# Loading q four tokens to a partition in two partition halves, with whole stores, in a linear-attention and feed-forward kernel

## Chip, cores and metric

One core of one Trainium2 chip. The metric is device time in microseconds (us). A run has a state: "fast", or "slow" where it lies over 1.5% above the fastest of its kernel; only fast runs are compared. A ratio below is the mean time of one kernel's fast runs over the mean of the other's fast runs of the same rounds, with a 95% interval; it is therefore not quite the ratio of the medians quoted beside it. "Span" is the time of the one profiled execution, some 2 to 3 us shorter than its timed run. In profile lines PE is TensorE, PEld its weight loads, DVE VectorE, ACT ScalarE, POOL GpSimd; `out<-in` names tiles, xN counts instructions, and L282 is a line of the kernel. "Granted clock" is the share of TensorE's full clock that it got.

## The reference

Decayed linear attention over blocks of 64 tokens, followed by a feed-forward layer whose activation is h + sin(ah)^2/a. There are 4 batches, 8 heads, 768 tokens and 64 dimensions a head; the feed-forward layer has 3072 rows, 512 wide, 2048 hidden.

```python
for b in range(nb):                                   # blocks of 64 tokens
    intra = np.einsum('bhic,bhjc->bhij', qb, kb) * Dmask[None]       # lam ** (i - j), i >= j
    intra = np.einsum('bhij,bhjd->bhid', intra, vb)
    inter = np.einsum('bhid,bhde->bhie', qb * lam_pow[None], kv_state)   # lam ** (i + 1)
    out[:, :, sl] = intra + inter
    kv_state = lam_block[None, :, None, None] * kv_state + np.einsum('bhsd,bhse->bhde', kb_dec, vb)
...
h = x @ w_in
s = np.sin(alpha * h)
return ((h + s * s / (alpha + 1e-09)) @ w_out).astype(np.float32)
```

## The kernel before

The work is cut into 24 units (256 tokens of one batch and four heads). A unit loads 256 KB each of q, k and v, scales q and k by powers of lam into bf16 (tiles QL and KD), transposes both, and runs the small matmuls of attention. Four units make one of six groups of 512 rows for the feed-forward layer. A list, ORDER, gives the program order of every operation; each engine takes its own in that order. Units 0 to 7 are transposed by TensorE, units 8 to 23 by DMA. All loads of q, k and v, all DMA transposes and nearly all stores are issued by one engine, the sync engine (SP; "SPq" in a profile is its DMA issues); I call that the sync queue. The DMAs that the sync engine and ScalarE issue take eight semaphores in turn, and a DMA waits until the eighth before it has landed: in the traces of the two kernels 255 of 260 DMAs whose eighth predecessor has a recorded landing carry that one's semaphore, and none was issued before that landing. I say that issues run free where those of a kind take their shortest time: in the kernel before a whole load's took 0.37 to 0.51 us in the first microseconds (up to 3.3 us) and again from 30.3 to 32.4 us.

```python
    def load(u, j, **_):                              # j: q, k or v
        ...
        tl = stagep.tile([P, HH, 2, D], FP32, name=f"st_{nm}")
        loads[u, j] = nc.sync.dma_start(              # 512 B pieces: two tokens of a head
            out=tl[:].rearrange("p h two e -> p h (two e)"),
            in_=src[b, hh * HH:(hh + 1) * HH, tp * W:(tp + 1) * W, :]
            .rearrange("h (p two) e -> p h (two e)", two=2))
        ...
    def turn_dma(u, j):
        nc.sync.dma_start_transpose(
            out=qkt[u][:, j].rearrange("p par hp i -> p (par hp) i"),
            in_=cast[u, "qk"[j]][:].rearrange("p par h e -> p (par h e)"))
    ...
    def outev(u, c, eng, **_):                        # attention result to the feed-forward input
        copy(eng, xt[g][:, 2 * hh:2 * hh + 2, bb, c, :],
             okv[u][c][:, 0:2 * P].rearrange("p (hp i) -> p hp i", hp=2))
    ...
    def store(g, m, par, **_):                        # even rows and odd rows: two half stores
        nc.sync.dma_start(out=out_rows(g, m)[par], in_=obs[g, m][par * D:(par + 1) * D, :])
```

Of the kernel before, what the change touches and what calls it, by code (L numbers as in the profile page):

```python
# [51 lines left out]
tdq.9:S s.8:T a.8.0:G sk.10:G st.0.0.0:S ld.12.0:S tdk.9:S st.0.0.1:S stt.1.6:V stt.1.7:V sin.1.8:A  # L52
sqr.1.8:A sin.1.9:A sin.1.10:A stt.1.8:V m.8.0:V f1.1.11:T:3 f1.1.12:T:0 f1.1.13:T:1 sq.11:G
tdq.10:S sin.1.11:A f1.1.14:T:4 ld.12.1:S ld.12.2:S ld.13.0:S sqr.1.9:V sqr.1.10:A sqr.1.11:G
stt.1.9:V stt.1.10:V sin.1.12:A sqr.1.12:G sin.1.13:A stt.1.11:V stt.1.12:V m.8.1:V sk.11:G
f1.1.15:T:2 cv.10:G sin.1.14:A sqr.1.13:A oi.8:T sin.1.15:A tdk.10:S f2.1.0.0:T:3 sqr.1.14:A sk.12:G
sq.12:G f2.1.0.1:T f2.1.0.2:T a.9.0:G sqr.1.15:A cv.11:A stt.1.13:V stt.1.14:V stt.1.15:V s.9:T
o.8:T tdq.11:S ld.13.1:S ld.13.2:S k.10:T:0,1 x.8.0:A x.8.1:A m.9.0:V tdk.11:S f2.1.0.3:T m.9.1:V
oi.9:T kc.10.0:A st.0.1.0:S ld.14.0:S kc.10.1:A o.9:T cv.12:A x.9.0:A s.10:T k.11:T:2,0 f2.1.1.0:T:1
m.10.0:V a.10.0:G x.9.1:A kc.11.0:A kc.11.1:A m.10.1:V oi.10:T k.12:T:2,0 n.6.0:G n.8.0:G n.9.0:G  # L60
s.11:T o.10:T kc.12.0:V f2.1.1.1:T ld.14.1:S m.11.0:V ld.14.2:S n.10.0:G x.10.0:V m.11.1:V
f2.1.1.2:T ld.15.0:S st.0.1.1:S ld.15.1:S tdq.12:S ld.15.2:S ld.16.0:S ld.16.1:S ld.16.2:S ld.17.0:S
oc.1.0:A kc.12.1:A x.10.1:A a.11.0:G sk.13:G cv.13:G oi.11:T o.11:T x.11.0:A sq.13:G f2.1.1.3:T
sq.14:G oc.1.1:A n.7.0:G x.11.1:V f1.2.0:T:6 sin.2.0:A f1.2.1:T:5 sin.2.1:A sqr.2.0:A stt.2.0:V
ld.17.1:S st.1.1.0:S a.6.1:G n.6.1:G sk.14:G ld.17.2:S st.0.3.0:S st.0.2.0:S f1.2.2:T:2 sin.2.2:A
sqr.2.1:A stt.2.1:V f1.2.3:T:7 sin.2.3:A f1.2.4:T:0 f1.2.5:T:3 sin.2.4:A f1.2.6:T:4 f1.2.7:T:5
sqr.2.2:G stt.2.2:V sqr.2.3:A a.5.1:G stt.2.3:V sin.2.5:A f1.2.8:T:6 f1.2.9:T:7 f1.2.10:T:1 sq.15:G
sk.15:G sqr.2.4:A sin.2.6:A sqr.2.5:A stt.2.4:V f2.1.2.0:T:0 stt.2.5:V cv.14:G f1.2.11:T:3 tdk.12:S
f1.2.12:T:2 sin.2.7:A f2.1.2.1:T st.0.2.1:S sin.2.8:A sqr.2.6:G sqr.2.7:A stt.2.6:V sin.2.9:A
stt.2.7:V sqr.2.8:G sin.2.10:A n.11.0:G stt.2.8:V sqr.2.9:A sqr.2.10:A stt.2.9:V stt.2.10:V sq.16:G  # L70
sin.2.11:A sqr.2.11:A tdq.13:S n.5.1:G tdk.13:S tdq.14:S st.0.3.1:S tdk.14:S a.7.1:G a.12.0:G s.12:T
k.13:T:6,7 kc.13.0:A sin.2.12:A kc.13.1:A sqr.2.12:A m.12.0:V m.12.1:V tdq.15:S f1.2.13:T:1
f2.1.2.2:T sin.2.13:A sqr.2.13:A oi.12:T s.13:T o.12:T stt.2.11:V f2.1.2.3:T a.13.0:G m.13.0:V
stt.2.12:V m.13.1:V stt.2.13:V x.12.0:A x.12.1:A f2.1.3.0:T:3 n.13.0:G n.7.1:G a.8.1:G oi.13:T
sk.16:G oc.1.2:A f1.2.14:T:2 o.13:T k.14:T:1,0 s.14:T sin.2.14:A x.13.0:V x.13.1:V m.14.0:V n.8.1:G
sq.17:G n.12.0:G kc.14.0:A f2.1.3.1:T m.14.1:V f2.1.3.2:T sqr.2.14:A a.14.0:G kc.14.1:A tdk.15:S
ld.18.0:S ld.18.1:S oi.14:T ld.18.2:S sq.18:G cv.15:A cv.16:G cv.17:A k.15:T:1,0 o.14:T s.15:T
tdq.16:S tdk.16:S stt.2.14:V kc.15.0:V x.14.0:V x.14.1:A f1.2.15:T:2 f2.1.3.3:T st.1.2.0:S a.15.0:G
m.15.0:V kc.15.1:V oi.15:T m.15.1:V ld.19.0:S ld.19.1:S ld.19.2:S s.16:T ld.20.0:S st.1.0.0:S o.15:T
x.15.0:V k.16:T:1 x.15.1:V sin.2.15:A sqr.2.15:A m.16.0:V oc.1.3:V stt.2.15:V a.11.1:G f2.2.0.0:T:0  # L80
f1.3.0:T:7 kc.16.0:A st.1.0.1:S ld.20.1:S m.16.1:V sin.3.0:A sqr.3.0:A f1.3.1:T:4 f1.3.2:T:6
sin.3.1:A f1.3.3:T:1 sqr.3.1:A sin.3.2:A sin.3.3:A f1.3.4:T:5 sin.3.4:A f1.3.5:T:2 f1.3.6:T:3
sk.17:G st.1.2.1:S ld.20.2:S sk.18:G sk.19:G f2.2.0.1:T f2.2.0.2:T a.9.1:G sq.19:G sq.20:G sqr.3.2:G
stt.3.0:V sqr.3.3:A stt.3.1:V a.16.0:G n.9.1:G sin.3.5:A sqr.3.4:A stt.3.2:V n.14.0:G n.15.0:G
sin.3.6:A stt.3.3:V stt.3.4:V sqr.3.5:A ld.21.0:S tdq.17:S tdk.17:S sqr.3.6:A cv.18:G tdq.18:S
tdk.18:S st.1.3.0:S f1.3.7:T:1 oi.16:T stt.3.5:V a.10.1:G s.17:T o.16:T x.16.0:V k.17:T:2 f2.2.0.3:T
cv.19:G m.17.0:V stt.3.6:V x.16.1:V kc.17.0:A f2.2.1.0:T:2 a.17.0:G n.10.1:G n.11.1:G sk.20:G
cv.20:G a.12.1:G f2.2.1.1:T tdq.19:S ld.21.1:S tdk.19:S ld.21.2:S ld.22.0:S st.1.1.1:S tdq.20:S
ld.22.1:S tdk.20:S m.17.1:V oi.17:T oc.2.0:V s.18:T st.1.3.1:S k.18:T:3 k.19:T:0 o.17:T kc.18.0:A
f2.2.1.2:T a.18.0:G sin.3.7:A x.17.0:A x.17.1:A n.12.1:G f2.2.1.3:T m.18.0:V m.18.1:V f1.3.8:T:3  # L90
oi.18:T oc.2.1:V sqr.3.7:A sin.3.8:A sqr.3.8:A sq.21:G ld.22.2:S ld.23.0:S st.2.1.0:S sk.21:G
kc.19.0:V s.19:T o.18:T k.20:T:2 kc.20.0:A m.19.0:V stt.3.7:V f1.3.9:T:0 m.19.1:V f1.3.10:T:4
sin.3.9:A stt.3.8:V a.19.0:G f1.3.11:T:1 st.2.0.0:S x.18.0:A x.18.1:V sqr.3.9:G sk.22:G sin.3.10:A
sqr.3.10:A f1.3.12:T:3 f1.3.13:T:2 oi.19:T stt.3.9:V sin.3.11:A sqr.3.11:A sin.3.12:A stt.3.10:V
cv.21:A f2.2.2.0:T:0 f2.2.2.1:T f2.2.2.2:T stt.3.11:V a.20.0:G sqr.3.12:A sin.3.13:A o.19:T s.20:T
f1.3.14:T:1 x.19.0:A sqr.3.13:G sq.22:G x.19.1:V sin.3.14:A m.20.0:V stt.3.12:V f1.3.15:T:6
f1.4.0:T:7 sqr.3.14:G stt.3.13:V stt.3.14:V sin.3.15:A sin.4.0:A sqr.3.15:A sqr.4.0:A stt.3.15:V
stt.4.0:V tdq.21:S st.2.0.1:S ld.23.1:S f2.2.2.3:T oc.2.2:A f1.4.1:T:4 a.13.1:G cv.22:G sin.4.1:A
sqr.4.1:G m.20.1:V f1.4.2:T:3 f1.4.3:T:0 sin.4.2:A sin.4.3:A sqr.4.2:A sqr.4.3:A sq.23:G
f2.2.3.0:T:1 f2.2.3.1:T tdk.21:S tdq.22:S ld.23.2:S oi.20:T n.13.1:G f2.2.3.2:T f2.2.3.3:T o.20:T  # L100
k.21:T:2 stt.4.1:V s.21:T stt.4.2:V stt.4.3:V kc.21.0:V oc.2.3:A f2.3.0.0:T:0 f1.4.4:T:3 f2.3.0.1:T
f1.4.5:T:2 x.20.0:A sin.4.4:A sin.4.5:A sqr.4.4:G a.15.1:G sqr.4.5:G stt.4.4:V m.21.0:V m.21.1:V
stt.4.5:V f1.4.6:T:1 sin.4.6:A tdk.22:S tdq.23:S sqr.4.6:A stt.4.6:V a.21.0:G st.2.3.0:S f2.3.0.2:T
f1.4.7:T:6 f1.4.8:T:3 f2.3.0.3:T sk.23:G oc.3.0:V f1.4.9:T:1 f1.4.10:T:5 f1.4.11:T:4 x.20.1:V
sin.4.7:A sin.4.8:A sqr.4.7:G sqr.4.8:G stt.4.7:V stt.4.8:V cv.23:A f1.4.12:T:2 tdk.23:S st.3.0.0:S
sin.4.9:A sqr.4.9:A stt.4.9:V sin.4.10:A sqr.4.10:G stt.4.10:V f2.3.1.0:T:3 f2.3.1.1:T n.15.1:G
sin.4.11:A st.2.2.0:S st.2.1.1:S sqr.4.11:A stt.4.11:V oi.21:T o.21:T k.22:T:0 k.23:T:1 s.22:T
x.21.0:V m.22.0:V x.21.1:V m.22.1:V f2.3.1.2:T f2.3.1.3:T oc.3.1:V st.2.3.1:S a.14.1:G n.14.1:G
kc.22.0:A a.22.0:G oi.22:T o.22:T s.23:T m.23.0:V f2.3.2.0:T:0 f2.3.2.1:T x.22.0:V kc.23.0:A
x.22.1:A m.23.1:V a.23.0:G oi.23:T f2.3.2.2:T f1.4.13:T:3 o.23:T x.23.0:V f1.4.14:T:4 x.23.1:V  # L110
f1.4.15:T:1 sin.4.12:A sqr.4.12:A stt.4.12:V sin.4.13:A st.2.2.1:S st.3.0.1:S sin.4.14:A sqr.4.13:A
# [8 lines left out]
stt.5.11:V stt.5.12:V st.4.0.0:S st.3.2.0:S st.3.2.1:S st.3.3.0:S st.3.1.0:S st.3.3.1:S f1.5.15:T:7  # L120
sin.5.13:A sin.5.14:A st.3.1.1:S f2.4.1.3:T oc.4.1:V sqr.5.13:A sqr.5.14:G sin.5.15:A stt.5.13:V
stt.5.14:V f2.4.2.0:T:4 st.4.0.1:S st.4.1.0:S st.4.1.1:S sqr.5.15:G stt.5.15:V f2.4.2.1:T f2.4.2.2:T
f2.4.2.3:T f2.4.3.0:T:0 f2.4.3.1:T f2.4.3.2:T f2.4.3.3:T f2.5.0.0:T:3 f2.5.0.1:T f2.5.0.2:T oc.4.2:V
oc.4.3:A st.4.3.0:S st.4.2.0:S st.4.3.1:S st.4.2.1:S f2.5.0.3:T oc.5.0:V st.5.0.0:S st.5.0.1:S
f2.5.1.0:T:2 f2.5.1.1:T f2.5.1.2:T f2.5.1.3:T f2.5.2.0:T:5 f2.5.2.1:T f2.5.2.2:T oc.5.1:V f2.5.2.3:T
st.5.1.0:S st.5.1.1:S lt.0:T:3 oc.5.2:V st.5.2.0:S lt.1:T:7 st.5.2.1:S ltc.0:A lt.2:T:5 ltc.1:A
ltc.2:V
"""

@with_exitstack  # L130
def kernel(
    ctx: ExitStack,
# [61 lines left out]
    nc.scalar.activation(out=warm[:], in_=warm[:], func=ACTF.Sin)  # L194
    alpha_r = consts.tile([NFC, P], FP32, name="alpha_r")
    nc.scalar.dma_start(out=alpha_r[:], in_=moe_alpha.rearrange("(f p) -> f p", p=P))

    pos = consts.tile([P, 1], FP32, name="pos")
    jt = consts.tile([P, 2], FP32, name="jt")
    for c in range(2):  # L200
# [54 lines left out]
    def load(u, j, **_):  # L255
# [7 lines left out]
        if (u, j) == (4, 0):  # L263
            after(loads[u, j], f1mm[HOLD])
# [25 lines left out]
    def table(eng, **_):  # L290
        tabs.append(ps.tile([P, 2, 2, H], FP32, name="tab", tag="h3", bufs=1))
        for j, t in enumerate((E, R)):
            copy(eng, tabs[0][:, j], t[:])
# [332 lines left out]
```

## Time and profile before

| what | before | how to read it |
|---|---|---|
| time | 217.48 us, median of 3 (215.25 to 217.53) | 216.37 with the run beside the changed kernel |
| span of the profile | 213.8 us | TensorE busy 204.0 us, 95% |
| first feed-forward matmul | 18.43 us | end of the start |
| last DMA transpose ends | 151 us | after it the sync queue only stores |
| sync queue issuing, 30 to 120 us | 89 to 94% of the time | issue times of the trace added up in 15 us windows |

### The profile page before, as it was taken

Reading aid. Unit: us, or ns where it says so; the run is one execution under the profiler, and the core shown is the slowest. Engines: PE = TensorE matmul, PEld = TensorE weight load, DVE = VectorE, ACT = ScalarE, POOL = GpSimd, SP = SyncE. Lnnn points to the kernel's source line nnn. Section 1 sums busy time; section 2 is a strip of 40 time slices with the busy share of each in tenths; the row PEclk is TensorE's granted clock in tenths of the full one; section 3 lists DMA queues with packets and bytes.
Section 4 is the critical chain, followed back from the end, with each engine's and each line's share of the span. In section 5 each row is a group of like instructions: output and inputs, shape, how many; then the busy total and the mean of one; then the engine's idle time right before and its main releaser. Section 6 shows DMA issues by size and latency. Waiting matters only on the chain.

```text
span 213.8 us, 5465 instructions
## 1 busy us (share of the span) xinstructions
PE 204.0 (95%) x2104; PEld 110.1 (51%) x2132; DVE 129.8 (61%) x235; ACT 123.5 (58%) x244; POOL 141.4 (66%) x208
## 2 busy tenths in 40 slices
PE   7989999999999999999799999999999999999993
PEld 5767544457744554455444554454454444444463
DVE  3885798159599845778667785626884626441120
ACT  3563984077899839986394496936635659131001
POOL 5488389689797999999898996709841728030000
PEclk9999999999999999999999999999999999999999
DMA  5999999999999999989899997520610000171624
GB/s 144 293 235 196 187 204 271 282 291 289 200 205 202 248 213 289 208 103 199 218 268 133 223 179 198 92 49 0 132 44 3 0 0 0 35 179 35 147 51 98
DMA packets 64009, 33.92 MB, mean 159 GB/s; under 512 B 19680, under 2 KB 61040, under 8 KB 63984
## 3 DMA queue, kind: packets, MB, share of 16 engines
q1 hardware_dynamic: 59568, 29.31, 62.5%
q0 software_dynamic: 4224, 4.19, 12.4%
q8 instruction: 16, 0.26, 0.5%
q10 hardware_dynamic: 192, 0.07, 0.2%
q14 instruction: 9, 0.07, 0.1%
HBM read 27.28 MB, written 6.29 MB: 157 GB/s over the span
## 4 chain that ended last, share of the span: by engine, by line
PE 67%; POOL 12%; DMA 10%; issue 3%; ACT 2%; SPq 2%; DVE 2%; POOLq 0%; ACTq 0%
PE ops L525 27%; PE hps L482 24%; DMA w_out_sb<-in_moe_w_out_dram 4%; PE bz L564 3%; DMA QT<-KD 2%; PE okv L460 2%; POOL KD L300 2%; POOL kvbd L425 2%; PE sp L368 2%; PE bz L588 2%; DMA st_v<-in_v_dram 2%; POOL QL L300 2%; POOL kvx L421 2%; PE pt L327 2%; SPq L259 2%
## 5 line engine op out<-in xcount | busy, mean ns | idle before, releaser
L482 PE MATMUL hps<-xt,w_in_sb 128*128 128x512 bf16 (+1 forms) x404 | 86.4, 362 | 0.6 <-issue 0.2
L525 PE MATMUL ops<-w_out_sb,gall 128*128 128x512 bf16 x352 | 83.2, 379 | 2.1 <-issue 1.3
L516 DVE SCALAR_TENSOR_TENSOR gall<-s,r_sb,hps 128x512 bf16<-128x512 bf16 x96 | 68.3, 744 | 23.3 <-POOL s L511 11.7
L502 ACT ACTIVATE s<-hps,alpha_sb 128x512 bf16<-128x512 f32 x96 | 63.2, 688 | 25.7 <-PE hps L482 25.1
L482 PEld LDWEIGHTS <-w_in_sb 128*128 128x128 bf16 x416 | 39.8, 98 | 40.6
L511 POOL TENSOR_TENSOR s<-s 128x512 bf16<-128x512 bf16 x35 | 36.3, 1045 | 36.3 <-ACT s L502 35.6
L525 PEld LDWEIGHTS <-gall 128*128 128x128 bf16 x368 | 34.6, 98 | 39.9 <-issue 0.6
L378 DVE TENSOR_TENSOR ST<-sp,mask 128x512 bf16<-128x512 f32 x48 | 31.9, 684 | 4.4 <-PE sp L368 4.2
L509 ACT ACTIVATE s<-s 128x512 bf16<-128x512 bf16 x51 | 31.6, 634 | 1.0 <-DVE gall L516 0.4
L284 DVE COPY ob<-ops 128x512 f32<-128x512 f32 (+1 forms) x13 | 8.6, 659 | 29.2 <-PE ops L525 23.6
L300 POOL TENSOR_TENSOR QL<-st_q,E 128x512 bf16<-128x512 f32 x23 | 23.9, 1042 | 3.6 <-DVE alpha_sb L574 2.2
L300 POOL TENSOR_TENSOR KD<-st_k,R 128x512 bf16<-128x512 f32 x22 | 22.9, 1042 | 3.5 <-DMA st_k<-in_k_dram 1.8
L425 POOL TENSOR_TENSOR kvbd<-kvx,LBD 128x256 bf16<-128x256 f32 x32 | 19.6, 612 | 2.5
L282 ACT COPY ob<-ops 128x512 f32<-128x512 f32 (+2 forms) x13 | 7.1, 547 | 22.4 <-PE ops L550 12.0
L282 ACT CAST xt<-okv 128x256 bf16<-128x256 f32 x29 | 9.8, 374 | 11.8 <-PE okv L460 11.8
L421 POOL TENSOR_TENSOR kvx<-kva,kvs 128x128 f32<-128x128 f32 x32 | 14.7, 460 | 1.2 <-ACT kva L282 1.0
L284 DVE CAST xt<-okv 128x256 bf16<-128x256 f32 x19 | 7.7, 420 | 11.5 <-PE okv L460 11.5
L282 ACT COPY kva<-kvp 128x128 f32<-128x128 f32 x26 | 6.4, 273 | 9.9 <-PE kvp L400 8.9
L368 PE MATMUL sp<-QT 64*64 64x128 bf16 x384 | 9.9, 219 | 1.3 <-DMA QT<-KD 1.3
L282 ACT COPY QT<-pt 128x512 bf16<-128x512 bf16 x9 | 5.2, 591 | 9.8 <-PE pt L327 9.7
L460 PE MATMUL okv<-ST,VB 64*64 64x128 bf16 x384 | 9.9, 220 | 0.0
L282 ACT CAST VB<-st_v 128x512 bf16<-128x512 f32 x14 | 8.6, 625 | 1.9 <-DMA st_v<-in_v_dram 1.8
(57 smaller groups left out, 127.1 us busy)
## 6 DMA issues: line engine op xcount, KB each, us to landing
st_q<-in_q_dram SPq DMA_DIRECT2D x24, 256.0 KB, 4.8
st_k<-in_k_dram SPq DMA_DIRECT2D x24, 256.0 KB, 5.0
st_v<-in_v_dram SPq DMA_DIRECT2D x24, 256.0 KB, 4.6
out_dram<-ob SPq DMA_DIRECT2D x46, 128.0 KB, 2.8
w_in_sb<-in_moe_w_in_dram POOLq DMA_DIRECT2D x4, 512.0 KB, 7.7
w_out_sb<-in_moe_w_out_dram POOLq DMA_DIRECT2D x4, 512.0 KB, 11.9
QT<-QL SPq DMA_TRANSPOSE x16, 4.1
QT<-KD SPq DMA_TRANSPOSE x16, 3.4
```

The lines of the kernel that those rows point to most:

```text
L282: nc.scalar.copy(out=out, in_=in_)
L284: eng.tensor_copy(out=out, in_=in_)
L300: eng.tensor_tensor(out=t[:], in0=stage[u, j][:].rearrange("p h two e -> p two h e"), in1=tab[:, :, hh * HH:(hh + 1) * HH].unsqueeze(3).to ...
L378: nc.vector.tensor_tensor(out=stm[u][:, hd], in0=sps[u][hd][:], in1=mask[:].unsqueeze(2).to_broadcast([P, 2, 2, P]), op=ALU.mult)
L421: eng.tensor_tensor(out=t[:], in0=x, in1=prev[:], op=ALU.add)
L425: eng.tensor_tensor(out=kvbd[u, c][:], in0=x.unsqueeze(2).to_broadcast([P, 2, 2, D]), in1=LBD[:, 2 * hh:2 * hh + 2, :].unsqueeze(3).to_bro ...
L482: f1mm[g, f] = nc.tensor.matmul(out=hps[g, f][:].rearrange("p (b i) -> p b i", b=2)[:, bs] .rearrange("p b i -> p (b i)"), lhsT=w_in_sb[:, ...
L502: nc.scalar.activation(out=s1[g, f][:], in_=hps[g, f][:], func=ACTF.Sin, scale=alpha_sb[:, f:f + 1])
L509: nc.scalar.activation(out=s2[g, f][:], in_=x[:], func=ACTF.Square)
L511: eng.tensor_tensor(out=s2[g, f][:], in0=x[:], in1=x[:], op=ALU.mult)
L516: nc.vector.scalar_tensor_tensor(out=gall[g][:, f, :], in0=s2.pop((g, f))[:], scalar=r_sb[:, f:f + 1], in1=hps.pop((g, f))[:], op0=ALU.mul ...
L525: nc.tensor.matmul(out=ops[g, m][:], lhsT=gall[g][:, f, m * P:(m + 1) * P], rhs=w_out_sb[:, f, :], start=(f == 0), stop=(f == NFC - 1))
```

## The change

Its intent: longer pieces for q (1 KB in place of 512 B, four tokens of a head to a partition), at the cost of cutting each q load into two DMAs, since two head pairs go to the two halves of the partitions; and, since the rows of a chunk come out in order, one contiguous store of 128 rows in place of two of 64. With four tokens to a partition, the power table of q has its own shape (EQ), the attention copies must permute rows, and the order of columns in QT changes.

```diff
+        if j == 0:
+            for hp in range(2):
+                loads[u, j] = nc.sync.dma_start(
+                    out=tl[hp * D:(hp + 1) * D].rearrange("p (hd i) two e -> p hd (i two e)", hd=2),
+                    in_=rows[2 * hp:2 * hp + 2].rearrange("hd (p t) e -> p hd (t e)", t=4))
... set-up
+    for hp in range(2):
+        sl = slice(hp * D, (hp + 1) * D)
+        nc.vector.tensor_copy(out=LQ[sl], in_=lam_v[sl, hp])
+    nc.gpsimd.tensor_tensor(out=EQ[:, :, 0, :], in0=LQ,
+                            in1=posq.unsqueeze(2).to_broadcast([P, 2, 2]), op=ALU.pow)
+    for i in range(3):
+        nc.vector.tensor_tensor(out=EQ[:, :, i + 1, :], in0=EQ[:, :, i, :], in1=LQ, op=ALU.mult)
... attention copies
-        copy(eng, xt[g][:, 2 * hh:2 * hh + 2, bb, c, :],
-             okv[u][c][:, 0:2 * P].rearrange("p (hp i) -> p hp i", hp=2))
+        copy(eng, xt[g][:, 2 * hh:2 * hh + 2, bb, c, :].rearrange("p hp (i t) -> p hp t i", t=4),
+             okv[u][c][:, 0:2 * P].rearrange("p (hp t i) -> p hp t i", hp=2, t=4))
... stores
-        nc.sync.dma_start(out=out_rows(g, m)[par], in_=obs[g, m][par * D:(par + 1) * D, :])
+        nc.sync.dma_start(out=out_rows(g, m), in_=obs[g, m][:])
... (score and inter-chunk matmuls read QT in the new order; the ORDER list loses the second half stores)
```

## The prediction

> **What bounds the kernel now.** I read the page first (busy time by engine, then the 40 slices), then the chain that ended last, then the busy time of each engine in chosen stretches, then the waits of TensorE, then the groups of instructions and the DMA issues.
>
> ```profile
> PE 204.0 (95%) x2104; PEld 110.1 (51%) x2132; DVE 129.8 (61%) x235; ACT 123.5 (58%) x244; POOL 141.4 (66%) x208
> DMA  5999999999999999989899997520610000171624
> ```
>
> TensorE is busy 95% of the span; no other engine is above 66%. The DMA row is nearly full for the first 25 slices (25 x 5.35 = 134 us) and mostly empty after. So two things compete as the bound of the first part: TensorE, and the 16 DMA engines. The stretches decide (columns: PE, PEld, DVE, ACT, POOL busy; granted clock; DMA share; GB/s; a share above 1 is transfers that overlap on one engine):
>
> ```profile
> 18.40:210.30 191.90, 187.81 (x1825) 98.20 (x1851) 116.85 (x196) 114.08 (x221) 129.01 (x184) 1.00 0.74 154
> 100.00:105.00 5.00, 3.94 (x103) 2.46 (x103) 2.96 (x7) 2.24 (x5) 4.84 (x9) 1.00 0.93 176
> 115.00:120.00 5.00, 4.40 (x104) 2.89 (x106) 3.76 (x7) 0.64 (x3) 4.50 (x9) 1.00 0.81 167
> ```
>
> From the first matmul of the feed-forward part (18.4 us) to the last matmul (210.3 us) TensorE is idle 191.90 - 187.81 = 4.1 us, of which 1.1 us lies in 100 to 105 and 0.6 us in 115 to 120. That 4.1 us is all that better transfers could give back after 18.4 us. The waits of TensorE say the same: only 1.3 us in total for the transposed tiles and 0.3 us for weights.
>
> ```profile
> PE sp L368 <- DMA QT<-KD: 1.3, 2, 1.0
> PE ops L525 <- DMA w_out_sb<-in_moe_w_out_dram: 0.3, 1, 0.3
> ```
>
> So the time is: a start of 18.4 us (much of TensorE's work there is warm-up filler), 188 us of matmuls that the change does not shorten, 4.1 us of gaps, and a tail of 213.8 - 210.3 = 3.5 us. The start is the part that transfers and set-up can move one for one. Its chain, from the view of the chain by time (start, length, what):
>
> ```profile
> 14.46 0.69 DVE ST L378
> 15.17 1.05 POOL KD L300
> 16.27 0.40 PE pt L327 x4
> 17.71 0.76 PE bz L588 x6
> 18.59 0.87 PE hps L482 x8
> ```
>
> The KD product at 15.17 is the k scaling of unit 3. The profile names a DVE instruction as what it waited for, but in the program order it waits on a DMA semaphore alone; I take it as released by the landing of unit 3's k, the eleventh large load.
>
> [...] The stores of before are exactly such halves (64 partitions, 2 KB rows). In a stretch with nothing but stores, and in one with nothing but loads of 128 partitions in 512 B pieces:
>
> ```profile
> 200.40:203.90 3.50, 3.50 (x18) 1.61 (x17) 0.74 (x2) 0.00 (x0) 0.00 (x0) 1.00 0.44 97
> 4.00:6.00 2.00, 2.00 (x13) 1.46 (x11) 1.41 (x9) 0.57 (x4) 1.51 (x1) 1.00 1.13 315
> ```
>
> Stores: 0.44 x 16 x 3.5 = 24.6 us of engine time for 97 x 3.5 = 340 KB, that is 166 rows of 2 KB at 148 ns, 13.8 GB/s for one engine, 221 GB/s for 16. Loads: 1.13 x 16 x 2 = 36.2 us for 630 KB, 1230 pieces at 29 ns, 17.4 GB/s, and 315 GB/s moved. Rows four times as long run slower[...]. [...]
>
> **The change part by part.**
>
> *q loads.* 24 loads of 256 KB in 512 B pieces become 48 of 128 KB in 1 KB pieces, each into one half of the partitions. Before, one took 256 KB / 315 GB/s = 0.83 us of the DMA engines. [...] it takes 256 KB / 221 = 1.19 us, so +0.35 us a unit: +1.4 us over the four units of the start, +8.5 us over all 24. [...] 24 more issues at the median of 0.58 us are 14 us of the sync queue.
>
> *Stores.* 46 half stores become 23 whole ones; 23 fewer issues at 0.59 us take 13.5 us off the same queue, so the queue's total is unchanged. [...] 256 KB goes from 1.19 to about 0.83 us: 23 x 0.35 = -8 us of DMA time. But they run from 58 us on, and the last 75 us have idle DMA engines: off the path. The last one still leaves one copy plus one landing (about 2 us) after the last matmul, so the tail stays at 3.5 us.
>
> *Set-up.* This is on the start's path. GpSimd must now do a second power before the old one. The old took 1.67 us for 8 values a partition; the new has 4, which I size at 0.9 us (half, plus something). VectorE gets two copies and three products more, five small instructions at about 0.17 us. Before, the power ran 3.84 to 5.51, and the first q product on VectorE began at 6.33. Now: copies to 4.1, new power to 5.0, old power to 6.7, then the last table product, reciprocal and the two table copies (0.8 us as before): first product at about 7.6, 1.3 us later. VectorE is nearly full from 5 to 14 us and then waits 0.97 us until 16.71 for unit 3's k, so about 0.3 us of the 1.3 gets through if that load does not move. If the load is later by 1.4 us, that hides the rest: the two are a maximum, not a sum.
>
> *Products, transposes, matmuls, copies.* The order of compute is as it was; only the second halves of the stores are gone from it. The q product keeps its 512 elements (1.04 us on GpSimd), the four transposes their 128x128 form, scores and inter-chunk matmuls their 128 columns (now four runs of 32 in place of two of 64), and the attention copies their 256 elements (0.37 and 0.42 us). I expect each within 3%.
>
> *Sum.* [...] Later: the two gaps may close by up to 1 us from quicker stores, or widen by as much because q and w_out share the DMA engines around 33 to 41 us, where the chain runs through 8.45 us of waiting for w_out. I take 0 for this, and +0.8 us for the start. The before runs lie at 215.25, 217.48 and 217.53, mean 216.8; adding 0.8 gives 217.6, and a little for the contention 218.
>
> **The rivals.**
>
> *A. Relief of the DMA engines.* They are full for 134 us; longer pieces and whole stores would shorten the loads and pull everything forward. For: the full DMA row, 10% of the chain on DMA. Against: only 4.1 us of TensorE idle after 18.4 us. Best case: half of that back and no delay at the start, about 214.5; 2% (4.3 us) would take all of it.
>
> *B. [...]* The wait for unit 3's k grows by 1.4 us, and w_out by about 1 us at 41 us, where TensorE has no other work in its order. For: the 148 ns of the half stores. [...] Result: 218 to 220.
>
> *C. The set-up chain.* It becomes the start's bound if the loads get quicker: +0.3 to +1.3 us, 217 to 218.
>
> *D. Strided operands.* If the runs of 32 columns slowed the score and inter-chunk matmuls (9.9 + 8.4 us busy) by half, +9 us. For: nothing in this trace; I give it one chance in twenty-five.
>
> **Range and chances.** A at one end (214.5) and B with a bad middle at the other (221) give 215 to 221. Run-to-run spread is itself 1%. Faster by over 2% needs all gaps closed: 0.06. Slower by over 2% needs B in full plus a new wait of some 2 us, or D: 0.10. Within 2%: 0.84.
>
> **What the profile after would show.** Right: TensorE busy still about 204 us; first feed-forward matmul 0.3 to 1.5 us after 18.4; the first q product on VectorE near 7.6; in store-only stretches over 18 GB/s for one engine in place of 13.8; sync queue issues within two of the old count; attention copies and score matmuls at their old durations. Wrong: a first feed-forward matmul before 18 us (then A holds in the start), stores still at 148 ns a row [...], score matmuls above 0.5 us for 16 (D), or TensorE idle after 18.4 us changed by over 2 us either way, which my sum sets to nothing.

## The result, and the profile after

The changed kernel takes 223.89 us (median of 4 runs, 222.77 to 226.36, the longest of them slow), the kernel before 216.37 (215.01 to 217.53) in the same rounds. The ratio is 1.033, interval 1.022 to 1.044: slower by over 2%, and above the predicted range of 215 to 221. The result is correct.

The changed kernel's page, busy time by engine and the DMA row of the 40 slices:

```profile
PE 206.7 (94%) x2104; PEld 110.6 (50%) x2132; DVE 134.7 (61%) x240; ACT 132.2 (60%) x244; POOL 143.2 (65%) x213
DMA  4999998999996799996779888631210000050312
```

Where is it lost? The changed kernel by stretches, with bounds moved by the delay so that they hold the same work (columns: stretch and length, then busy time of PE, PEld, DVE, ACT, POOL, granted clock, DMA share, GB/s):

```profile
20.62:65.90 45.28, 41.28 (x452) 23.79 (x457) 27.86 (x51) 29.01 (x56) 32.03 (x44) 1.00 1.10 217
65.90:132.55 66.65, 63.55 (x790) 33.19 (x802) 49.30 (x80) 50.56 (x97) 60.86 (x96) 1.00 0.93 206
132.55:217.85 85.30, 84.72 (x585) 41.65 (x592) 43.42 (x66) 41.30 (x71) 35.84 (x45) 1.00 0.24 71
```

The same stretches of the kernel before:

```profile
18.40:60.00 41.60, 40.85 (x453) 23.84 (x458) 27.66 (x52) 26.79 (x56) 32.46 (x45) 1.00 1.17 242
60.00:125.00 65.00, 62.24 (x790) 32.73 (x802) 47.29 (x80) 47.12 (x97) 60.59 (x95) 1.00 1.03 208
125.00:210.30 85.30, 84.72 (x585) 41.63 (x592) 41.90 (x66) 40.18 (x71) 35.97 (x45) 1.00 0.31 70
```

The start, which the tables leave out, is 2.2 us longer (20.62 against 18.40), the first stretch shown 3.7 us, the second 1.65 us, and the last is equal to the hundredth. Nothing is lost once loads and transposes are over; so the slower attention copies, shown below, are not what the last 85 us feel, and the stores there do not matter either. In the first stretch TensorE's idle time (length less busy) goes from 0.75 to 4.00 us, in the second from 2.76 to 3.10; 1.7 us more are recorded as busy in small matmuls.

The same division can be read more finely from the start of the first sine of each feed-forward group, k-th against k-th. This table also holds the experiments, which are explained further on (each row: delay against the profile before, us; times in the head are those of before):

| kernel | group 0, 21.3 | group 1, 55.4 | group 2, 79.9 | group 3, 107.1 | group 4, 134.1 | group 5, 166.0 |
|---|---|---|---|---|---|---|
| changed | +2.2 | +5.9 | +7.0 | +7.0 | +7.5 | +7.6 |
| e2_setup | +0.2 | -0.1 | +1.5 | -0.1 | +0.6 | +0.6 |
| e1_copy | +1.3 | +1.9 | +5.1 | +6.5 | +6.8 | +6.8 |
| e3_split | +0.2 | +0.3 | +2.0 | +4.1 | +4.2 | +4.2 |
| e4_half | +1.1 | +2.8 | +9.1 | +9.9 | +11.8 | +11.8 |
| e5_store | +0.5 | +2.5 | +2.5 | +1.4 | +1.0 | +1.0 |
| e20_drain10 | -0.2 | +0.1 | +5.3 | +5.7 | +6.0 | +6.0 |
| e22_drain18 | +1.1 | +1.5 | +5.9 | +10.1 | +10.5 | +10.5 |
| e19_halfst | +2.3 | +6.5 | +8.4 | +13.1 | +13.9 | +13.9 |

Each row is one profile. e2_setup and e5_store, whose ratios are 1.002 and 1.000, stand at +1.5 and +2.5 at one group and lose most of it again, so a delay of that size at a single group shows nothing.

What does TensorE wait for? The waits of TensorE in the changed kernel (line, what ended the wait: us in total, times, longest), and one of GpSimd:

```profile
PE ops L559 <- DMA w_out_sb<-in_moe_w_out_dram: 2.3, 1, 2.3
PE okv L479 <- ACT xt L302: 1.1, 3, 0.4
PE sp L401 <- DMA QT<-KD: 1.0, 3, 0.4
PE kvp L433 <- POOL kvs L466: 0.8, 1, 0.8
```

```profile
POOL QL L321 <- DMA st_q<-in_q_dram: 8.3, 6, 3.2
```

GpSimd, which makes QL, waited 1.4 us for q in the kernel before and waits 8.3 us now. The chain that ended last names it too. Its pieces around 40 us in the changed kernel (start, length, what):

```profile
36.98 1.68 SPq L282
38.66 0.04 issue
38.70 8.83 DMA st_q<-in_q_dram
47.53 0.02 issue
47.55 0.02 SPq L276
47.57 0.03 issue
47.60 0.98 SPq L276
48.58 0.04 issue
48.62 5.90 DMA st_q<-in_q_dram
54.52 0.03 issue
54.55 0.04 POOLq L321
```

From 37 to 54.5 us the end of the kernel hangs on one queue: issue, landing of a q half, an issue that had waited for that landing (the turn among eight), landing of another q half. Of these 17.5 us, 14.7 are the landing of two q halves. In the kernel before the same chain, once w_out has landed at 40.95 and up to 60 us, is made of TensorE's own matmuls and transposes alone. Issue by issue, in the sync queue's timeline of the kernel before (start, length, what, count), and then of the changed kernel:

```profile
43.18 1.03 SPq L259 DMA_DIRECT2D st_q<-in_q_dram  x1
45.97 0.71 SPq L259 DMA_DIRECT2D st_q<-in_q_dram  x1
48.47 0.72 SPq L259 DMA_DIRECT2D st_q<-in_q_dram  x1
```

```profile
43.48 2.54 SPq L276 DMA_DIRECT2D st_q<-in_q_dram  x2
47.60 1.63 SPq L276 DMA_DIRECT2D st_q<-in_q_dram  x2
50.60 1.77 SPq L276 DMA_DIRECT2D st_q<-in_q_dram  x2
53.83 1.81 SPq L276 DMA_DIRECT2D st_q<-in_q_dram  x2
```

A unit's loads pass every 2.5 to 2.8 us before and every 3.0 to 4.1 us now. And the groups of instructions of the attention copies, before, then after (busy, mean ns of one | idle before):

```profile
L282 ACT CAST xt<-okv 128x256 bf16<-128x256 f32 x29 | 9.8, 374 | 11.8 <-PE okv L460 11.8
L284 DVE CAST xt<-okv 128x256 bf16<-128x256 f32 x19 | 7.7, 420 | 11.5 <-PE okv L460 11.5
```

```profile
L302 ACT CAST xt<-okv 128x256 bf16<-128x256 f32 x29 | 19.7, 770 | 11.2 <-PE okv L493 11.2
L304 DVE CAST xt<-okv 128x256 bf16<-128x256 f32 x19 | 13.3, 732 | 10.6 <-PE okv L493 10.6
```

They nearly doubled, where the prediction had them "within 3%".

### The profile page after: what moved, and what is told of

It reads as the page before. It is cut to its first block, busy times and chain, and to the rows that moved or that the text cites.

```text
span 221.0 us, 5465 instructions
## 1 busy us (share of the span) xinstructions
PE 206.7 (94%) x2104; PEld 110.6 (50%) x2132; DVE 134.7 (61%) x240; ACT 132.2 (60%) x244; POOL 143.2 (65%) x213
## 4 chain that ended last, share of the span: by engine, by line
PE 52%; DMA 15%; POOL 11%; SPq 7%; ACT 5%; issue 5%; DVE 4%; POOLq 0%; ACTq 0%
PE hps L516 23%; PE ops L559 22%; DMA st_q<-in_q_dram 9%; DMA QT<-KD 6%; SPq L276 4%; SPq L282 3%; ACT s L536 3%; POOL QL L321 3%; POOL KD L332 2%; PE okv L493 2%; POOL s L545 2%; PE ops L584 2%; PE sp L401 1%; ACT xt L302 1%; POOL kvs L466 1%
## 5 line engine op out<-in xcount | busy, mean ns | idle before, releaser
L321 POOL TENSOR_TENSOR QL<-st_q,EQ 128x512 bf16<-128x512 f32 x23 | 23.9, 1045 | 8.8 <-DMA st_q<-in_q_dram 8.3
L302 ACT CAST xt<-okv 128x256 bf16<-128x256 f32 x29 | 19.7, 770 | 11.2 <-PE okv L493 11.2
L304 DVE CAST xt<-okv 128x256 bf16<-128x256 f32 x19 | 13.3, 732 | 10.6 <-PE okv L493 10.6
L302 ACT COPY kva<-kvp 128x128 f32<-128x128 f32 x26 | 6.9, 291 | 8.5 <-PE kvp L433 7.5
L479 PE MATMUL okv<-QT,kvbd 128*128 128x128 bf16 x80 | 8.7, 219 | 1.2 <-ACT xt L302 1.1
```

What stands on the lines that cost most here:

```text
L302: nc.scalar.copy(out=out, in_=in_)
L304: eng.tensor_copy(out=out, in_=in_)
L321: eng.tensor_tensor(out=t[:], in0=stage[u, 0][:].rearrange("p (hd i) two e -> p (i two) hd e", hd=2), in1=tab[:, hh].unsqueeze(3).to_broad ...
```

## The experiments

At first four theories stood against each other; the expectations use short names for them. *Copies*: the strided attention copies are on the path, ten and six microseconds of engine time more. *Set-up*: the longer chain ahead of the first product delays the start and carries through. *Half partitions* (PORTS in the expectations): q into half of the partitions lands more slowly. *Queue*: more issues on the sync queue, whatever they move. The calls in which kernels ran together each had their own runs of the kernel before (medians 216.3, 217.2, 216.1, 217.0 and 215.9).

| run | what it is | median us | ratio to before, 95% interval |
|---|---|---|---|
| changed | | 223.89 | 1.033 [1.022, 1.044] |
| e1_copy | changed, copies write in order | 223.59 | 1.032 [1.027, 1.038] |
| e2_setup | before, set-up of the change added | 217.45 | 1.002 [0.995, 1.009] |
| e3_split | before, q in two DMAs by heads | 219.48 | 1.010 [1.004, 1.017] |
| e4_half | before, q in two DMAs by partition halves | 228.37 | 1.053 [1.046, 1.059] |
| e5_store | before, whole stores | 216.65 | 1.000 [0.995, 1.004] |
| e6_tiny | before, a tiny DMA after each q | 224.14 | 1.033 [1.027, 1.038] |
| e7_stact | changed, stores from ScalarE | 229.71 | 1.064 [1.054, 1.074] |
| e10_best | before, whole stores from ScalarE | 223.09 | 1.027 [1.022, 1.033] |
| e8_kvpair | changed, k and v of two units in one DMA | 223.0 | 1.036 [1.028, 1.044] |
| e16_bkvpair | before, the same | 218.76 | 1.015 [1.009, 1.022] |
| e11_pairall | before, q, k and v of two units in one DMA | 217.37 | 1.008 [0.999, 1.016] |
| e14_pairbest | the same with whole stores | 220.32 | 1.019 [1.009, 1.029] |
| e17_drain4 | before, sync engine held up 4 steps a unit | 217.92 | 1.002 [0.995, 1.010] |
| e20_drain10 | the same, 10 steps | 220.8 | 1.017 [1.009, 1.024] |
| e22_drain18 | the same, 18 steps | 226.79 | 1.053 [1.045, 1.061] |
| e18_splitdrain | e3_split, 4 steps | 224.53 | 1.035 [1.027, 1.043] |
| e19_halfst | changed, stores halved again | 229.1 | 1.056 [1.049, 1.063] |
| e21_tiny1 | before, a one-row tiny DMA after each q | 223.85 | 1.030 [1.021, 1.039] |

All gave correct results.

### e1_copy: the copies write in order

```diff
-             okv[u][c][:, 0:2 * P].rearrange("p (hp t i) -> p hp t i", hp=2, t=4))
+             okv[u][c][:, 0:2 * P].rearrange("p (hp t i) -> p hp i t", hp=2, t=4))
  (and the write side in its natural order: the stride is on the PSUM read in place of the SBUF write)
```

> The changed kernel, with the attention copies written in order and PSUM read at a stride of 32 values instead; all else as changed. In the changed kernel these copies took 0.77 us (ScalarE) and 0.73 us (VectorE) in place of 0.37 and 0.42 of before. Theory COPY (the strided write doubles them, and TensorE waits for the bank they free): they fall back to about 0.4 us, the first feed-forward matmul comes some 0.7 us earlier, and the whole gains 1 to 3 us, to 220 to 222 (223.9 changed). Theory LOAD (q's extra issues are the cause): copies may be quick again, but the time stays within 1 us of the changed kernel. If the strided read of PSUM is as slow as the strided write, the copies stay at 0.7 us and nothing is learnt of the path.

The copies went back to 374 and 420 ns, exactly as before the change, and the kernel took 223.59 us, as slow as the changed one. The table of delays shows why: the start comes 0.9 us and group 1 four microseconds earlier, and by group 3 all but half a microsecond of it is lost again (0.8 us at the end). TensorE now waits for transposed tiles:

```profile
PE sp L401 <- DMA QT<-KD: 5.3, 5, 1.7
```

So the copies are not the cause of the total. They had only stood in front of another delay. What they cost at the start, 0.9 us, does not add to the total. The stretch whose chain is shown above (group 0 to group 1) loses only 0.6 us here, against 3.7 in the changed kernel; e1_copy loses its time between groups 1 and 3, and so do e20_drain10 and e22_drain18 below.

### e2_setup: the set-up alone

```diff
+    nc.gpsimd.tensor_tensor(out=XQ[:, :, 0, :], in0=XL, in1=..., op=ALU.pow)
+    ... (two copies before it, three products after it, as the change has them; results not used)
```

> The kernel before with the added set-up alone (a second power of 4 values on GpSimd before the old one, five small VectorE instructions; their results unused). Theory SETUP: the first q product moves from 6.3 to 7.6 us, the first feed-forward matmul by 0.3 to 1.3 us, and this stays to the end, 216.6 to 217.6. If the sync queue alone bounds the end, the delay of the start is taken up before 130 us and the time stays at 216.3 +- 0.4.

Ratio 1.002, interval across 1; delays of 0.2 us at group 0 and 0.6 at group 4. The set-up is worth little: the slack of the start takes nearly all of its delay up.

### e3_split and e4_half: q in two DMAs, cut by heads or by partition halves

```diff
-        loads[u, j] = nc.sync.dma_start(out=..., in_=...)
+        for ps_, hs in CUTS:      # q only
+            loads[u, j] = nc.sync.dma_start(out=to[ps_, hs], in_=rows[ps_, hs])
  e3: CUTS = [(slice(0, P), slice(0, 2)), (slice(0, P), slice(2, 4))]
  e4: CUTS = [(slice(0, D), slice(0, HH)), (slice(D, P), slice(0, HH))]
```

> The kernel before, with each q load cut into two DMAs of two heads each, over all 128 partitions, 512 B pieces as before; nothing else. Adds 24 issues on the sync queue and uses up the eight DMA semaphores faster. Theory LOAD: this alone loses most: the first feed-forward matmul moves by 0.5 to 1.5 us, the loss between the first and second feed-forward stages is 2 us or more, the time 219 to 222. Theory COPY or SETUP: at most 1 us slower than before (216.4), up to 217.5.

> As e3_split, but cut by partitions: two DMAs of 64 partitions with all four heads, 512 B pieces. Theory PORTS [...]: q pieces of 512 B take over 36 ns where DMA is full, and this is 1 us or more slower than e3_split. Theory LOAD by issues alone: within 0.5 us of e3_split.

Same count of DMAs, same bytes, same 512 B pieces: 1.0% against 5.3%. This is the largest single effect, larger than the whole change. My first reading was the data: half the partitions take it more slowly. But the two also differ in issue time (0.47 us for an issue cut by heads, 0.61 to 0.63 for one cut by halves, where issues run free), so the pair alone does not decide. The data did become dearer, as the half-partition theory expected (over 36 ns a piece). From 40 to 50 us a piece of 512 B took 39.6 ns in mean in e4_half (packet records of the traces), against 29.7 in e3_split and 30.5 in the kernel before. The same stretch in the kernel before, the changed kernel, e4_half and e22_drain18 (last two columns: DMA share, GB/s):

```profile
40.00:50.00 10.00, 9.41 (x150) 5.38 (x151) 5.20 (x10) 5.44 (x13) 7.71 (x10) 1.00 1.12 296
40.00:50.00 10.00, 7.61 (x62) 3.81 (x61) 2.33 (x4) 1.72 (x4) 5.22 (x6) 1.00 1.16 253
40.00:50.00 10.00, 8.56 (x100) 4.57 (x100) 3.16 (x6) 3.48 (x8) 4.95 (x6) 1.00 1.16 235
40.00:50.00 10.00, 9.13 (x103) 4.86 (x103) 3.76 (x8) 4.17 (x9) 7.27 (x9) 1.00 1.09 290
```

A byte costs the DMA engines some 20% more time in the changed kernel (part of it is w_out, which still lands there) and 30% more in e4_half; with drains (e22_drain18, below) it costs what it did before. The waits of GpSimd for q and of TensorE for K transposes in e4_half:

```profile
POOL QL L304 <- DMA st_q<-in_q_dram: 11.1, 7, 3.2
```

```profile
PE sp L372 <- DMA QT<-KD: 3.7, 3, 1.9
```

### e5_store: the stores alone

```diff
-        nc.sync.dma_start(out=out_rows(g, m)[par], in_=obs[g, m][par * D:(par + 1) * D, :])
+        if par == 0:
+            nc.sync.dma_start(out=out_rows(g, m), in_=obs[g, m][:])
  (rows of a chunk in order, so the attention copy permutes at a stride of 2 elements)
```

> The kernel before with the store part alone: one store of contiguous rows for each row tile, and attention copies that put the two token parities in order (write stride of 2 values, 4 bytes); q loads and set-up as before. Theory COPY: copies slower than 0.42 and 0.37 us, if the cost depends on the stride perhaps 0.5, and the time up by 0 to 1.5 us. Stores themselves: 2 KB rows at about 85 ns as in the changed kernel in place of 148, which is worth nothing to the time. If the copies stay as quick as before, the time is 216 +- 1.

Ratio 1.000, within half a per cent: 23 issues fewer on the sync queue and quicker stores give the kernel before nothing. Keep this for e19_halfst. The copies took 449 and 442 ns at this stride of 4 bytes, against 374 and 420 in order.

### e6_tiny: one more DMA, without data

```diff
+        if j == 0:
+            nc.sync.dma_start(out=tiny[:, u % H:u % H + 1], in_=lam[u % H:u % H + 1].partition_broadcast(P))
```

> The kernel before, plus one tiny DMA (512 B in all) on the sync queue after each unit's q load: 24 more issues and semaphore turns, no data to speak of. Theory ISSUE (from 30 to 135 us the sync queue is filled by the issuing itself, so that each added issue delays every later load and transpose): 24 x 0.4 us are 9.6 us of issue, and with what other issues give back (as in e3_split) 3 to 8 us slower than before, 219 to 224. Theory PORTS (only the rate into half the partitions counts): within 1 us of before, 216.3.

128 pieces of 4 B after each q load cost 3.3%, as much as the whole change. So data are not needed for a loss of this size; the queue theory stood.

### e7_stact and e10_best: stores from another engine

```diff
-        nc.sync.dma_start(out=out_rows(g, m), in_=obs[g, m][:])
+        nc.scalar.dma_start(out=out_rows(g, m), in_=obs[g, m][:])
  e7: in the changed kernel.  e10: in the kernel before, with whole stores and in-order copies
```

> The changed kernel with all its 23 stores issued from the ScalarE queue in place of the sync queue; the same DMAs otherwise. Theory ISSUE: takes about 12 x 0.6 us of issue off the sync queue before its last transpose, so 3 to 6 us come back of the 7.5: 218 to 221, with the second sine stage no earlier but the later ones earlier. Theory PORTS: the time stays at 223 to 224, as no byte moves otherwise. Possible harm: ScalarE waits at a store for a copy of VectorE; up to 2 us.

> A candidate that might beat both: q loads, set-up and mask of the kernel before; whole stores of contiguous rows, issued from the ScalarE queue; attention copies written in order, PSUM read at the stride that puts the two parities in order. Theory ISSUE: it takes some 25 store issues (14 us) off the sync queue while that is full; the gaps of TensorE after 18.4 us (4.1 us) shrink, 213 to 215.5. If before is bound by TensorE and not by the queue, 216 +- 1.

Both failed, and as tests of the queue they are confounded: a store issued by ScalarE waits for the DMA eight before it, which is mostly one of the sync engine's, and ScalarE, which has the sines to do, stands still. In e7 it waits 3.1 us for a transpose of QL and 5.5 us for a v load ahead of sines, and TensorE then 6.6 us for VectorE's step after the sine (gall), which comes late. They say nothing for or against the theory, only that this way out is closed here.

### e8_kvpair, e16_bkvpair, e11_pairall, e14_pairbest: fewer, larger loads

```diff
+        tl = stagep.tile([P, 2, HH, 2, D], FP32, name=f"st_{nm}", bufs=RING // 2)
+        loads[u, j] = nc.sync.dma_start(              # even units from unit 4 on: 512 KB
+            out=tl[:].rearrange("p g h two e -> p (g h) (two e)"),
+            in_=src[b, :, tp * W:(tp + 1) * W, :].rearrange("h (p two) e -> p h (two e)", two=2))
  e8: k and v in the changed kernel.  e16: k and v in the kernel before.  e11: q, k and v there.  e14: e11 + whole stores, in-order copies
```

> The changed kernel, with k and v of two units (all eight heads of a token range) in one DMA of 512 KB each from unit 4 on; q as changed, same bytes, same partition halves, same stores, same set-up and strided copies. 20 fewer issues on the sync queue, which then has about as many load issues as the kernel before. Theory ISSUE: the queue is no longer the bound; most of the 7.5 us come back, 215 to 219. Theory PORTS (half-partition q transfers are slow in themselves) or COPY: stays at 222 to 224.

> The control for e8_kvpair: the kernel before with the same pairing of k and v from unit 4 on, its q loads whole and its stores halved. Theory ISSUE: the queue has room, the gaps of TensorE close, 213.5 to 216. What is left between this and e8_kvpair is what halved q loads, strided copies and set-up cost once the queue has room; theory PORTS expects 5 us or more, theory ISSUE under 3 us.

> The kernel before with q, k and v of two units in one DMA of 512 KB each from unit 4 on: 30 fewer issues. Might beat both kernels. Theory ISSUE: 213 to 216; the start is as before, the gain is bounded by the 4.1 us that TensorE was idle after 18.4 us. Possible harm: the first half of a pair lands later, up to 1 us in the stretch after 30 us.

> As e11_pairall, plus the store part of the change (whole stores of contiguous rows on the sync queue) with attention copies written in order (PSUM read at a stride): 53 fewer issues on the sync queue than before. If the queue still counts after e11_pairall, this is 0.5 to 2 us quicker than it; if TensorE bounds by then, the same.

Twenty issues fewer did not bring the changed kernel back (1.036), so the bare count of issues is not the measure. The control shows a cost of its own: pairing k and v costs the kernel before 1.5%. TensorE waits 4.0 us for K transposes in e8_kvpair, 3.0 of them at once; I read that as a transpose held up by 512 KB issued ahead of it, which was not tested by itself. What the change costs on top of pairing is about 2.0% (1.036 over 1.015), 4.2 us; the expectation had under 3 us for the queue and 5 or more for half partitions, so the pair decides nothing. None of the four beats the kernel before; e11_pairall is the only one whose interval touches 1.

### e17_drain4, e20_drain10, e22_drain18: the sync engine held up, no DMA added

```diff
+        if j == 0:
+            for i in range(4):        # 10 in e20, 18 in e22
+                nc.sync.drain()
```

A drain here is an empty instruction on the sync engine; the edit adds no DMA, and so no turn among the eight. Nor did the drains wait for transfers: in e22_drain18 the gap from a q issue to the next issue was 1.11 to 1.18 us in all but four of the 24 units, where issues ran free and where they did not.

> The kernel before with four empty instructions (drains) on the sync engine after each q load: it occupies the queue that issues the transfers, with no data, no descriptor and no semaphore turn. Their length is not known to me; the start of the trace will show it (I guess 0.05 to 0.1 us each, so 0.2 to 0.4 us a unit, 5 to 10 us over all). Theory 'occupied queue' (the queue from which everything is issued in order has no slack between 30 and 125 us): the end moves by a good part of that, +2 to +5 us. Theory 'turns and data' (only another transfer among the eight in flight, or the half-partition data, costs): 0 +- 1 us, because the queue waits for landings anyway and the idle instructions fall into those waits.

> The same with ten a unit, meant to be near the 0.51 us that the tiny transfer's issue took in its run, or somewhat above. 'Occupied queue': as much as the tiny transfer cost, +7 us, or more if they are longer. 'Turns and data': within 1 us of the kernel before, up to some 0.2 us at the start.

> The kernel before with eighteen drains after each q load. Ten lengthened the time to the second q issue by 0.52 us and cost 1.7%; eighteen (66 ns each) should lengthen it by about 1.05 us, which is what the half-partition cuts of q do (1.04 to 1.10). If the engine's occupation by itself is what the half cut costs: +4.5 to +5.5%, 226 to 229. If the slower data of half the partitions, or the second turn among the eight in flight, carries a good part: +2.5 to +4%, 222 to 225.5.

First the dose. In the first microseconds issues run free (0.41 to 0.51 us for a load of the kernel before), so the start of the second q issue tells how long a unit holds the queue. The sync queue's timeline of the kernel before, then of e22_drain18, then of the changed kernel:

```profile
1.20 0.41 SPq L259 DMA_DIRECT2D st_q<-in_q_dram  x1
...
2.75 0.51 SPq L259 DMA_DIRECT2D st_q<-in_q_dram  x1
```

```profile
1.21 0.41 SPq L259 DMA_DIRECT2D st_q<-in_q_dram  x1
2.73 0.37 SPq L259 DMA_DIRECT2D st_k<-in_k_dram  x1
3.15 0.50 SPq L259 DMA_DIRECT2D st_v<-in_v_dram  x1
3.69 0.51 SPq L259 DMA_DIRECT2D st_q<-in_q_dram  x1
```

```profile
1.18 1.38 SPq L276 DMA_DIRECT2D st_q<-in_q_dram  x2
2.60 0.60 SPq L282 DMA_DIRECT2D st_k<-in_k_dram  x1
3.24 0.51 SPq L282 DMA_DIRECT2D st_v<-in_v_dram  x1
3.79 1.25 SPq L276 DMA_DIRECT2D st_q<-in_q_dram  x2
```

From 2.75 it moves to 3.69 with eighteen drains (+0.94 us a unit) and to 3.79 in the changed kernel (+1.04); to 2.96 with four drains, 3.27 with ten, 3.23 in e3_split, 3.85 in e4_half.

Then the answer. Four drains (24 x 0.21 = 5.0 us of queue time in all) cost nothing that can be told from zero, where the queue theory had expected 2 to 5 us. Ten (24 x 0.52 = 12.5 us) cost 1.7%, 3.6 us, half of what that theory expected. Eighteen (24 x 0.94 = 22.6 us) cost 5.3%, 11.4 us: as much as e4_half at nearly the same dose (+1.10 us a unit), with every q load whole, in 128 partitions, and no DMA added. Time on the sync engine alone is enough for a loss of this size. It is not proportional: the first 5 us are free, and between ten and eighteen drains 10 us more of the queue make 7.8 us more of the kernel. Part of the 11.4 us can be the clock: the fast runs of e22_drain18 had 0.975 to 0.992, those of the kernel before 0.997 to 1.000, and a clock lower by 0.8% over 204 us of busy TensorE is an estimated 1.6 us. It is not the whole: the run at 0.975 took 226.4 us and the others 226.1 to 228.7, and e18_splitdrain, next, had 0.999 or more in four of its five runs.

### e18_splitdrain: the head cut with the half cut's queue time

```diff
  e3_split, and after the two q DMAs:
+            for i in range(4):
+                nc.sync.drain()
```

> The kernel with q cut by heads (two transfers a unit, all partitions) plus four empty instructions a unit, which brings the queue's time for a q pair from about 0.94 us near the 1.22 us that a pair cut by partition halves takes. If the half cut costs more than the head cut because its issues are longer: near the half cut, 226 to 228. If it costs more because half the partitions take the data slower: as the head cut alone, 219 to 220.5.

1.035 against 1.010 for the head cut alone. The dose reached was +0.73 us a unit (second q issue at 3.48), two thirds of the half cut's, and the cost is two thirds of the half cut's as well (7.6 of 11.4 us). Neither expectation is met to the letter, since the dose fell short; but a loss that grows like this needs no slower data (a piece took 30.0 ns in mean here and 29.9 in e3_split).

### e19_halfst: the changed kernel with its stores halved again

```diff
-        nc.sync.dma_start(out=out_rows(g, m), in_=obs[g, m][:])
+        for par in range(2):
+            nc.sync.dma_start(out=out_rows(g, m)[par * D:(par + 1) * D],
+                              in_=obs[g, m][par * D:(par + 1) * D, :])
```

> The changed kernel with each store cut again into two halves of 64 partitions (contiguous rows, both issued where the one was): undoes the saving of 20 issues and the quicker store data, keeps all else. By the prediction's account (store issues saved pay for the q issues added) this would cost as much as the change saved, some +13 us of the queue's time and by the occupied-queue theory several us: 228 to 232. If the stores lie outside the stretch that matters, or their time was never on the path (as the kernel with whole stores alone suggested): within 1.5 us of the changed kernel, 223 to 225.

229.1 us, 1.056 against 1.033. The store part, worth nothing in the kernel before (e5_store), is worth 2.2% once q is cut. The delay arises between groups 2 and 3, 80 to 107 us, and not at the end of the kernel. Halving brings back two things at once, more issues and slower rows (145 ns for 2 KB against 88 at the end of the kernel), and this run does not part them.

### e21_tiny1: one row in place of 128 small pieces

```diff
-            nc.sync.dma_start(out=tiny[:, ...], in_=lam[...].partition_broadcast(P))
+            nc.sync.dma_start(out=tiny[0:1, :], in_=lam[None, :])
```

> The kernel with a tiny transfer after each q load, but now of one row of 32 B to one partition in place of 128 pieces of 4 B. If the 128 small pieces [...] are why the tiny transfer cost 3.3% where the head cut, with the same queue time and as many transfers, cost 1.0%: down to 1 to 1.7%, 219 to 220.5. If it is the transfer's turn as such, or its two microseconds of latency: 3% again, 223 to 224.

Still 1.030, but this run tests something else than was meant. Every unit writes the same row of the same tile, so each tiny DMA waits for the one before it to land. From the waits of the sync engine (the profiled run was slow, but the waits are there from the start, before the second and third tiny issue at 4.3 and 7.5 us):

```profile
SPq L267 <- DMA tiny<-in_lam_dram: 9.2, 10, 1.9
```

With these 9.2 us and the 0.32 us a unit that its issue adds, the queue is held for some 17 us, which by the drains costs about 7 us. So e21_tiny1 is explained by the queue, and whether the 128 pieces are what made e6_tiny dear stays open: there the sync engine has no such wait, and its cost is some 4 us more than its queue time, which e3_split with as many DMAs does not show.

### Reading the doses together

Take what the drains say as a curve of its own: 0 us of queue time costs 0, 5.0 costs 0.5, 12.5 costs 3.6, 22.6 costs 11.4 us (ratio less one, times 216.5). Then work out the queue time of the others: the shift of the second q issue times 24; and for stores only those issued ahead of the last transpose, because later ones hold up nothing (by program order 20 half stores before, 11 whole ones after, 22 halves in e19_halfst). At the medians 0.59 and 0.42 us of an issue, that is 11.8 us before and 4.6 us after.

| kernel | queue time added, us | from the drains' curve | measured |
|---|---|---|---|
| e5_store | -7.2 | 0 | 0.0 |
| e3_split | 24 x 0.48 = 11.5 | 3.2 | 2.3 |
| e18_splitdrain | 24 x 0.73 = 17.5 | 7.5 | 7.6 |
| changed | 24 x 1.04 - 7.2 = 17.8 | 7.7 | 7.2 |
| e19_halfst | 24 x 1.06 + 1.2 = 26.6 | 14.5 | 12.1 |
| e4_half | 24 x 1.10 = 26.4 | 14.3 | 11.4 |
| e6_tiny | 24 x 0.48 = 11.5 | 3.2 | 7.1 |
| e21_tiny1 | 24 x 0.32 + 9.2 = 16.9 | 7.0 | 6.5 |

(The values of the curve's column for e19_halfst and e4_half are extended beyond eighteen drains at the slope between ten and eighteen.) Seven of the eight rows lie within 3 us of the curve; e6_tiny does not. This table was made after the runs, so it is a summary and not a test.

That the changed kernel lies within half a microsecond is partly luck. The first unit is not typical: its q pair took 1.38 us and later ones 1.25, and its whole load 0.41 and later ones 0.51. From second to third q issue, a unit takes 2.48 us in the changed kernel, 2.52 in e4_half, 2.49 in e19_halfst, 2.37 in e18_splitdrain and 2.59 in e22_drain18. In the kernel before issues no longer run free there (0.69 us each for k and v); I estimate 1.55 + 0.10 = 1.65 us, since with drains the second unit is 0.10 to 0.12 longer than the first. Read so, the curve gives 10.1 us for e4_half, 10.5 for e19_halfst and 7.3 for e18_splitdrain (20.9, 21.4 and 17.3 us of queue time), near what was measured, but for the changed kernel 24 x 0.83 - 7.2 = 12.7 us of queue time and 3.8 us, half of its loss. So by this reckoning the queue's time explains between half and all of the change's loss; the dearer data of q in halves is the rival for the rest, and no run here has that data without the longer issues.

## Why the prediction was wrong

The step that failed is this one: "24 more issues at the median of 0.58 us are 14 us of the sync queue", against stores where "23 fewer issues at 0.59 us take 13.5 us off the same queue, so the queue's total is unchanged", and from there "I take 0 for this" for everything after 18.4 us. Three things were wrong in it.

- *The size of the addition.* A q half holds the queue about 0.6 us where issues run free (1.25 for the pair), and a whole load 0.51; with the k issue behind them a unit's loads hold it 0.83 to 1.04 us longer, 20 to 25 us in all and not 14. I had priced one more issue a unit at the median of a whole load, and not the dearer issue of both halves.
- *Where the saving falls.* Of the 23 store issues saved, only 9 lie ahead of the last transpose; the rest belong to a stretch where nothing waits for the queue. The saving that counts is 7.2 us. So the total was +13 to +18 us in the part that matters, where the prediction had half a microsecond.
- *What the queue is worth.* I named two bounds, TensorE and the DMA engines, and took the sync queue for a number to be balanced. It issues during 89 to 94% of the time from 30 to 120 us, and e22_drain18 shows that holding it longer is paid for at some 0.8 us a microsecond once the slack is gone. The prediction read the full DMA row as the data's limit and never added up the issues.

The other steps, in order:

- *"That 4.1 us is all that better transfers could give back"* was right for gains (e5_store gains nothing), and I let it stand as if it also bounded losses. It does not: TensorE's idle time after the start went from 4.1 to 7.7 us, which the prediction had itself named as a sign of being wrong.
- *Start, +0.8 us*, taken between 0.3 for the set-up alone and 1.4 with q at the rate of the half stores. Measured +2.2. The first product on VectorE came at 7.66 us where 7.6 was predicted, so the set-up was worked out rightly, and it is worth 0.2 us at group 0 (e2_setup). The copies carry 0.9 of it (e1_copy against the changed kernel), and the prediction had left them out. In the rest the chain of the changed kernel runs through issues without a gap from 0.7 to 9.4 us and then through 5.6 us of landing of a q half; the twelfth load is issued at 10.84 us in place of 9.34. The 1.3 us left are near those 1.4 us (4 x 0.35), but e22_drain18, with whole loads, has 1.1 too, so that agreement does not show that rate to be the cause.
- *"+0.35 us a unit"* of DMA time sets 221 GB/s of engine time, measured on the half stores, against 315 GB/s moved by overlapping loads; by engine time for both (17.4 GB/s x 16 = 278) it would be 0.25. That q in halves would move at the rate of the half stores, and whole stores at that of the loads, was an estimate. Measured over the whole run (packet records), a 1 KB piece of q took 63.7 ns and two of 512 B before 62.0, 0.03 us a unit, while the pieces of k and v went from 31.0 to 33.0, another 0.13. The doubled piece saved nothing either.
- *"I expect each within 3%"* was wrong for the attention copies (374 to 770 ns on ScalarE, 420 to 732 on VectorE) and right for the score matmuls (219 ns before and after) and for the q product (1042 and 1045 ns). It is the wrong step with the largest number, 15.5 us of engine time, and yet not the cause: e1_copy takes it away and gains nothing.
- *Stores no longer limited by the half.* Right. In a stretch of the changed kernel that holds stores only,

```profile
207.00:211.50 4.50, 4.45 (x22) 2.03 (x21) 1.23 (x2) 0.00 (x0) 0.00 (x0) 1.00 0.16 60
```

  0.16 x 16 x 4.5 = 11.5 us of engine time move 60 x 4.5 = 270 KB, 132 rows of 2 KB: 87 ns a row where half partitions took 148. The whole stores also write adjacent rows; but e19_halfst, with halves of adjacent rows, has 145 ns again. So the 145 to 148 ns went with the halves, whatever the order of the rows, as rival B's evidence needed. The tail is unchanged, as predicted.
- *The rivals.* A did not show. B named the right place (TensorE's wait for w_out went from 0.3 to 2.3 us), but at most half the size (218 to 220). Its carrier, slower data of the halves, is in the trace (40 to 50 us above), yet is not needed for a loss of this size, as e22_drain18 and e18_splitdrain show; B did not have the issue of a half, which is dear too. C is e2_setup, 0.2 us at group 0. D is refuted by the 219 ns.

Not settled: how much of the cost of the changed kernel and of e4_half is slower data; e6_tiny's excess of some 4 us; and how the delay divides, within the changed kernel's middle, between issue time and the turn among eight that its chain shows at 47.5 us. No version tried beats the kernel before.

## What to carry to other kernels

Where loads, DMA transposes and stores all leave from one engine, add up the issues of that engine by stretch before cutting a transfer in two: price a cut by the issue time of the new shape, taken from the trace where issues run free (here 1.25 us for two q halves against 0.51 for a whole load), and count a saved issue only if it lies ahead of the last transfer that somebody waits for. This queue answered with a bend: its first 5 us were free (and removing 7 us gained nothing, as with the stores alone), and past ten drains each microsecond cost some three quarters of its length. Empty instructions on the issuing engine are a clean way to measure where the bend is, since they move no data; a small probe transfer is not, when each must wait for the last (9.2 us in e21_tiny1). And an instruction group that doubles in time needs its own test before it is called the cause.

## Issue, cast and store times measured here

- One issue on the sync engine, in the first microseconds of each trace: 0.51 us for 128 partitions x 4 x 512 B (kernel before), 0.47 for 128 x 2 x 512 B (e3_split), 0.60 to 0.63 for 64 partitions with those 128 KB, in 512 B pieces (e4_half) or 1 KB pieces (changed kernel), 0.25 to 0.40 for one row of 32 B (e21_tiny1). A DMA transpose took 1.2 us at the median of 32 (kernel before).
- The DMA engines move 256 KB in 0.83 us, an estimate at the 315 GB/s of the kernel before from 4 to 6 us. Holding the issuing engine 0.94 us a unit longer cost 5.3% by itself (e22_drain18), with every load whole; the cut into halves cost 5.3% (e4_half).
- A cast from PSUM that writes at a stride of 4 elements (8 B) took 770 ns on ScalarE and 732 on VectorE (changed kernel), at a stride of 2 elements 449 and 442 (e5_store), in order 374 and 420 (kernel before). With a stride of 128 B on the PSUM read side it took 374 and 420 too (e1_copy).
- With stores issued from ScalarE the time was 2.7% (e10_best, whole stores included) and 6.4% (e7_stact, the whole change included) above the kernel before; in e7_stact ScalarE stood waiting 3.1 and 5.5 us for DMAs of the sync engine.
